# Weights ahead of batch 0, kv in the banks of the turned queries, gated relu chunks: one change to a cosformer attention kernel

## The chip, the cores and the metric

The kernel runs on one core of one Trainium2 chip. The metric is the device time of one execution in microseconds (us). A run is called slow when it is over 1.5% above the fastest of the same kernel.

PE is the matmul engine and PEld its weight load. DVE is the vector engine, ACT the scalar engine, and Pool the GpSimd engine, which here also issues the loads. A "turn" is a transpose by matmul: the result appears in PSUM, the memory that PE writes, and another engine copies it into SBUF. A name like L281 is a line of the kernel that the text speaks of; the same statement has another number in each kernel.

## The reference

Linear attention with cosine and sine weights over 8 batches, then a feed-forward layer with softplus, cut to what matters:

```python
# q, k, v: (8 batches, 8 heads, 576 positions, 64)
q_p, k_p = phi(q), phi(k)     # phi: relu, then [r * cos(pos), r * sin(pos)]
kv  = einsum('bhsf,bhsd->bhfd', k_p, v)
z   = k_p.sum(over positions)
x   = (q_p @ kv) / (q_p @ z + 1e-6)            # 4608 tokens of 512
h   = x @ w_in                                 # 512 -> 2048
out = (maximum(h, 0) + log1p(exp(-abs(h)))) @ w_out
```

Where every h is small, the last line is close to `ln 2 * sum(w_out) + x @ (w_in @ w_out) / 2`. The kernel computes that: it folds the two weights into one 512 x 512 matrix `W_c`. It squares x and w_in to check at the end that h was small enough, and holds a slow branch for the other case.

## The kernel before

The 4608 tokens are 36 tiles of 128. Two batches of 576 make nine tiles: four of each, and one that holds the last 64 tokens of both. A batch's work:

```python
def relu(b):                                   # once a batch, on Pool
    nc.gpsimd.tensor_copy(gate, vcs_bufs[(b - 1) % 2][:, 3, T - 1, 1, VW - 2 :])
    for hq in range(2):
        relu_q(b, hq, nc.gpsimd)               # q_sb -> q_r, a pool of 2 buffers
    relu_k(b, nc.gpsimd)

def turn_queries(b, n):                        # nine times a batch
    ...
    ps = qt_ps.tile([128, 512], F32, tag="qt") # qt_ps: bufs=2, one bank each
    ...                                        # two matmuls with diag (cos and sin) into ps
    nc.scalar.copy(dst, ps.rearrange("p (j c s) -> p j c s", j=2, c=4))

def key_values(b, hq):                         # twice a batch
    kv = big_ps.tile([128, 2, 512], F32, tag="big", name="kv_ps")   # shared with attend
    ...                                        # 36 matmuls, then two ACT copies into blk
```

The `gate` copy reads the last value that a scaling wrote, and the relu stands behind it on Pool. So Pool's relu starts after that scaling on DVE: in the trace of before, a gate copy waits 4.96 us for the scaling and runs at 62.80, and the relu follows at 62.95. And the main loop, one tile at a time:

```python
for j, i in enumerate(mine):
    attend(i)                                  # q.kv, q.z; DVE divides: x
    for hq, c in itertools.islice(scales, 2 if j == 0 else 1):
        scale_values(b + 1, hq, c)             # v * cos, v * sin on DVE
    if j == 2 and b + 2 < B:
        relu(b + 2)
    if more and j >= last - 1:
        key_values(b + 1, j - last + 1)
    some(1)                                    # a query turn of batch b + 1
    if i - 1 >= 4:
        turn_x(i - 1)                          # x turned, copied by ACT, squared by ACT
    some(1 if j < last else 9)
    if i - 2 >= 4:
        emit(i - 2)                            # x @ W_c + bias, stored
```

Batch 0 and its four tiles come first, while the weights arrive. Then come all squares and the fold of the weights, then batch 1.

Of the kernel before, what the change touches and what calls it, by code (L numbers as in the profile page):

```python
# [21 lines left out]
def kernel(  # L22
# [19 lines left out]
    T = 9  # L42
# [11 lines left out]
    qt_ps = ctx.enter_context(tc.tile_pool(name="qt_ps", bufs=2, space=PSUM))  # L54
# [4 lines left out]
    def view(ap, *dims, offset=0):  # L59
        return bass.AP(  # L60
            tensor=ap.tensor, offset=ap.offset + offset,
            ap=[list(ap.ap[0])] + [list(d) for d in dims],
        )

# [12 lines left out]
    warm = singles.tile([128, 512], BF16)  # L77
    nc.vector.memset(warm, 1.0)
    load(0, "q", 0)
    load(0, "q", 1)  # L80


    idx_i = singles.tile([128, T], mybir.dt.int32)
# [4 lines left out]
    for part in range(2):  # L88
        load(0, "k", part)
        load(0, "v", part)  # L90

    xT_all = singles.tile([128, N_TOK // 128, KO, 128], BF16)
    w_in_sb = xT_all[:, 4 : 4 + D_FF // 128].rearrange("p n g t -> p (n g t)").rearrange(
        "p (ko f) -> p ko f", ko=KO
    )
    w_out_sb = singles.tile([128, FO, D_MODEL], BF16)
    for ko in range(KO):
        nc.gpsimd.dma_start(w_in_sb[:, ko, :], moe_w_in[ko * 128 : (ko + 1) * 128, :])
    w_out_r = moe_w_out.rearrange("(fo p) m -> p fo m", p=128)
    for f in range(0, FO, 4):  # L100
        nc.gpsimd.dma_start(w_out_sb[:, f : f + 4, :], w_out_r[:, f : f + 4, :])
    for b in (1, 2, 3):
        for name in ("q", "k", "v"):
            load(b, name)

    ones = singles.tile([128, 128], F32)
    nc.vector.memset(ones, 1.0)
    blk_bufs = []
    for r in range(3):
        blk = singles.tile([128, 2, 2, 2, C], BF16, name=f"kvblk{r}")  # L110
        nc.vector.memset(blk, 0.0)
        blk_bufs.append(blk)
# [11 lines left out]
    nc.scalar.copy(cs_wide, view(cs_col, [1, 2 * T], [0, D]))  # L124
    diag = singles.tile([128, T, 2, 128], BF16)
    for t in range(T):
        for c in range(2):
            nc.vector.tensor_scalar_mul(diag[:, t, c, :], ident, cs_col[:, c, t : t + 1])
    perm = singles.tile([128, 128], BF16)
    nc.vector.tensor_copy(view(perm, [2, 64], [1, 2]), view(ident, [1, 64], [64, 2]))  # L130
# [5 lines left out]
    def turn_w_in(ko, half):  # L136
        n = (2 * ko + half) % 3
        pool, tag = (xt_ps, "xt") if n == 0 else (qt_ps, "qt")
        ps = pool.tile([128, 8, 128], BF16, tag=tag, name="wT_ps")
        for j in range(8):  # L140
            ft = 8 * half + j
            nc.tensor.matmul(
                ps[:, j, :], w_in_sb[:, ko, ft * 128 : (ft + 1) * 128], ident,
                is_transpose=True, start=True, stop=True, skip_group_check=True,
            )
        dst = view(
            w_inT, [D_MODEL, 8], [128, 2], [1, 64],
            offset=8 * half * D_MODEL + 256 * (ko // 2) + 64 * (ko % 2),
        )
        src = ps.rearrange("p f (h d) -> p f h d", h=2)  # L150
        if half:
            nc.scalar.copy(dst, src)  # L152
        else:
            nc.vector.tensor_copy(dst, src)

    def fold(pair, quarter, ps):
        for ft in range(4 * quarter, 4 * quarter + 4):
            for j in range(2):
                g = 2 * pair + j
                nc.tensor.matmul(  # L160
                    ps[:, j, :], w_inT[:, ft, g * 128 : (g + 1) * 128], w_out_sb[:, ft, :],
                    start=(ft == 0), stop=(ft == FO - 1),
                )
# [32 lines left out]


    VW = D + 2
    vcs_bufs = []
    for r in range(2):  # L200
        vcs = singles.tile([128, 4, T, 2, VW], BF16, name=f"vcs{r}")
        vcs_bufs.append(vcs)

    def mark_values(r):
        for hp in range(4):
            at = 0 if hp % 2 else D
            nc.vector.tensor_copy(
                vcs_bufs[r][:, hp, :, :, at : at + 2], view(cs_col, [1, T], [T, 2], [0, 2])
            )

    def scale_values(b, hq, c):
        vcs = vcs_bufs[b % 2]
        nc.vector.tensor_mul(  # L213
            view(vcs, [T * 2 * VW + 2, 2], [2 * VW, T], [1, D],
                 offset=2 * hq * T * 2 * VW + c * VW),
            kqv[b, "v"][:, 2 * hq : 2 * hq + 2],
            view(cs_wide, [0, 2], [D, T], [1, D], offset=c * T * D),
        )

    def key_values(b, hq):  # L220
        vcs, blk, k_r = vcs_bufs[b % 2], blk_bufs[b % 3], kqv[b, "k"]
        kv = big_ps.tile([128, 2, 512], F32, tag="big", name="kv_ps")
# [18 lines left out]
    TURNS = [(hq, tp) for tp in range(TP) for hq in range(2)] + [(0, TP)]  # L241

    def turn_queries(b, n):
        hq, tp = TURNS[n]
        q_r = q_rs[b]
        if n == 0:
            qTs[b] = work.tile([128, 2, 4, S], BF16, tag="qT", name="qT", bufs=3)
        qT = qTs[b]
        ps = qt_ps.tile([128, 512], F32, tag="qt")
# [10 lines left out]
        nc.scalar.copy(dst, ps.rearrange("p (j c s) -> p j c s", j=2, c=4))  # L260


    tiles = []
    for b in range(B):
        tiles += [[(b, 128 * tp, 128, 0)] for tp in range(TP)]
        if b % 2:
            tiles.append([(b - 1, 512, 64, 0), (b, 512, 64, 64)])
    xs = {}

    x_norm = singles.tile([128, len(tiles)], F32)  # L270
    w_norm = singles.tile([128, FO], F32)

    def attend(n):
        num = big_ps.tile([128, 4, 256], F32, tag="big", name="num_ps")
        for g in range(4):
# [12 lines left out]
        x = outs.tile([128, 4, 2, D], BF16, tag="x", bufs=3)  # L288
        nc.vector.tensor_mul(  # L289
            x, view(num, [256, 4], [66, 2], [1, D]), view(rden, [2, 4], [1, 2], [0, D])  # L290
        )
        xs[n] = x

    def turn_x(n):
        x = xs.pop(n)
        ps = xt_ps.tile([128, 4, 128], F32, tag="xt", name="xT_ps")
        for g in range(4):
            nc.tensor.matmul(  # L298
                ps[:, g, :], x[:, g, :, :], perm if len(tiles[n]) == 1 else ident, start=True, stop=True, skip_group_check=True,
            )  # L300
        nc.scalar.copy(xT_all[:, n], ps)  # L301
        square = outs.tile([128, D_MODEL], BF16, tag="square", name="square", bufs=1)
        nc.scalar.activation(square, x, ACT.Square, bias=zero_b, accum_out=x_norm[:, n : n + 1])  # L303
# [9 lines left out]
    def emit(n):  # L313
        ps = o_ps.tile([128, D_MODEL], F32, tag="o", name="o_ps")
# [7 lines left out]
    def spin(count):  # L322
        ps = qt_ps.tile([128, 512], F32, tag="qt", name="spin_ps")
        for _ in range(count):
            nc.tensor.matmul(ps, warm[:, :128], warm, start=True, stop=True, skip_group_check=True)

    def fetch(b):
        for name in ("q", "k", "v"):
            load(b, name)

    gate = singles.tile([128, 2], BF16)

    def relu(b):

        nc.gpsimd.tensor_copy(gate, vcs_bufs[(b - 1) % 2][:, 3, T - 1, 1, VW - 2 :])  # L335
        for hq in range(2):
            relu_q(b, hq, nc.gpsimd)
        relu_k(b, nc.gpsimd)

    spin(16)  # L340
    for hq in range(2):
        relu_q(0, hq, nc.vector)
    mark_values(0)
    for hq in range(2):
        relu_k(0, nc.vector, slice(2 * hq, 2 * hq + 2))
        for c in range(2):
            scale_values(0, hq, c)
    for n in range(9):
        turn_queries(0, n)
    key_values(0, 0)  # L350
    spin(2)
    key_values(0, 1)
    spin(2)
    w_turns = iter([(ko, half) for ko in range(KO) for half in range(2)])
    for n in range(4):
        attend(n)
        turn_w_in(*next(w_turns))
        if n:
            turn_x(n - 1)
    mark_values(1)  # L360
    for ko, half in w_turns:
        turn_w_in(ko, half)
        if (ko, half) == (2, 0):
            turn_x(3)
    for ft in range(FO):
        square = outs.tile([128, D_MODEL], BF16, tag="square", name="square", bufs=1)
        nc.scalar.activation(  # L367
            square, w_inT[:, ft, :], ACT.Square, bias=zero_b, accum_out=w_norm[:, ft : ft + 1]
        )
    wc_ps = [big_ps.tile([128, 2, D_MODEL], F32, tag="big", name=f"wc_ps{r}") for r in range(2)]  # L370
    for quarter in range(4):
        sum_w_out(quarter)
        for pair in range(2):
            fold(pair, quarter, wc_ps[pair])
    for hq in range(2):
        relu_q(1, hq, nc.vector)
# [3 lines left out]
    bias()  # L380
    relu_k(1, nc.vector)
    for n in range(9):
        turn_queries(1, n)
        if n % 2:
            emit(n // 2)
            scale_values(1, n // 4, n // 2 % 2)
    for hq in range(2):
        key_values(1, hq)
    fetch(4)
    relu(2)  # L390

    n = 4
    for b in range(1, B):
        mine = [i for i in range(n, len(tiles)) if tiles[i][-1][0] == b]
        last = len(mine) - 1
        more = b + 1 < B
        turns = iter(range(9))

        def some(count):
            for _ in range(count):  # L400
                t = next(turns, None) if more else None
# [112 lines left out]
```

## Time and profile before

| | before |
|---|---|
| median of the first 3 runs | 149.9 us (149.88 to 150.5) |
| span of the profiled run, granted clock | 148.7 us, 0.971 |
| busy: PE, DVE, ACT, Pool | 81%, 73%, 76%, 36% |
| loads done | about 108 us |
| nine tiles in the middle | 24.45 us |
| x of tiles 0, 4, 9, 18, 27, 31, 35 starts at | 17.9, 53.3, 68.4, 92.8, 117.3, 129.0, 136.2 us |

The last row follows one DVE instruction, the multiplication that makes x, through the timeline. It happens once a tile, so it serves as the tiles' clock.

### The profile page before, as it was taken

How to read it: one execution, taken by the hardware profiler on the slowest of the kernel's cores; microseconds unless marked ns; L12 is line 12 of the kernel's file. 1: busy time of each engine (PE TensorE's matmuls, PEld its weight loads, DVE VectorE, ACT ScalarE, POOL GpSimd, SP SyncE). 2: the span in 40 equal slices, each digit the busy share in tenths (PEclk: the TensorE clock that was granted, in tenths of full speed). 3: DMA queues.
4: the chain of work that ended last, by engine and by line, in shares of the span. 5: the costliest groups of instructions: out<-in, count | busy, mean ns of one | idle time of the engine just before them, and what ended most of it. 6: DMA issues, size and time to landing. Idle time of an engine off the chain costs nothing.

```text
span 148.7 us, 3802 instructions
## 1 busy us (share of the span) xinstructions
PE 119.9 (81%) x1482; PEld 75.6 (51%) x1482; DVE 108.9 (73%) x237; ACT 113.7 (76%) x255; POOL 53.0 (36%) x67
## 2 busy tenths in 40 slices
PE   6966875999967728798979899897899988999510
PEld 2323665444434507566657567575567755664100
DVE  6867494699467579978967986994998798599420
ACT  3468298999995626899899889989988989967300
POOL 6965132231300095196079059219009200000000
PEclk9999999999999986999999999999999999999985
DMA  1999999999999999999999999999942324144430
GB/s 21 181 179 216 213 213 202 209 204 209 207 207 208 267 266 209 208 208 265 239 250 256 239 239 269 228 256 249 241 171 82 142 74 109 61 155 152 153 90 4
DMA packets 20678, 28.07 MB, mean 189 GB/s; under 512 B 1200, under 2 KB 15536, under 8 KB 20656
## 3 DMA queue, kind: packets, MB, share of 16 engines
q0 software_dynamic: 15408, 18.35, 71.8%
q1 hardware_dynamic: 5248, 9.44, 18.8%
q8 instruction: 12, 0.20, 0.5%
q14 instruction: 10, 0.08, 0.2%
HBM read 36.70 MB, written 9.44 MB: 310 GB/s over the span
## 4 chain that ended last, share of the span: by engine, by line
PE 33%; DVE 25%; ACT 23%; issue 7%; DMA 5%; POOL 3%; DVEq 0%; POOLq 0%
PE o_ps L316 17%; DVE o_sb L318 11%; ACT square L367 9%; DVE vcs L213 8%; DMA v_sb<-in_v_dram 5%; PE kv_ps L227 5%; PE num_ps L279 4%; PE ps L252 4%; DVE x L289 3%; ACT square L303 3%; ACT qT L260 3%; ACT w_inT L152 3%; PE xT_ps L298 2%; ACT xT_all L301 2%; ACT kvblk L234 2%
## 5 line engine op out<-in xcount | busy, mean ns | idle before, releaser
L260 ACT CAST qT<-ps 128x512 bf16<-128x512 f32 x72 | 40.6, 592 | 11.3 <-PE ps L252 10.9
L316 PE MATMUL o_ps<-W_c,xT_all 128*128 128x512 bf16 x144 | 36.9, 378 | 5.1 <-DVE o_sb L318 3.5
L318 DVE TENSOR_TENSOR o_sb<-o_ps,b_bc 128x512 f32<-128x512 f32 x36 | 24.8, 688 | 13.4 <-PE o_ps L316 13.3
L252 PE MATMUL ps<-diag,q_r 128*128 128x256 bf16 x144 | 27.7, 279 | 8.1 <-ACT qT L260 4.6
L213 DVE TENSOR_TENSOR vcs<-v_sb,cs_wide 128x1152 bf16<-128x1152 bf16 x32 | 27.9, 871 | 2.4 <-ACT qT L260 1.2
L289 DVE TENSOR_TENSOR x<-num_ps,rden 128x512 bf16<-128x512 f32 x36 | 24.9, 692 | 3.3
L303 ACT ACTIVATE square<-x,zero_b 128x512 bf16<-128x512 bf16 x36 | 26.6, 739 | 0.0
L279 PEld LDWEIGHTS <-qT 128*128 128x128 bf16 (+1 forms) x320 | 19.6, 101 | 9.0 <-DVE x L289 1.9
L279 PE MATMUL num_ps<-kvblk,qT 128*128 128x130 bf16 (+1 forms) x320 | 23.4, 223 | 0.6 <-ACT kvblk L234 0.5
L301 ACT CAST xT_all<-xT_ps 128x512 bf16<-128x512 f32 x36 | 21.5, 596 | 3.0 <-PE xT_ps L298 3.0
L316 PEld LDWEIGHTS <-xT_all 128*128 128x128 bf16 x144 | 13.8, 97 | 17.1 <-issue 7.9
L252 PEld LDWEIGHTS <-q_r 128*128 128x128 bf16 x144 | 11.8, 99 | 15.0 <-issue 8.0
L234 ACT CAST kvblk<-kv_ps 64x260 bf16<-64x260 f32 x32 | 12.0, 375 | 6.0 <-PE kv_ps L227 5.7
L298 PE MATMUL xT_ps<-perm,x 128*128 128x128 bf16 x128 | 12.6, 222 | 3.0 <-DVE x L289 1.2
L160 PE MATMUL wc_ps<-w_out_sb,w_inT 128*128 128x512 bf16 x64 | 14.0, 379 | 0.1
L192 POOL TENSOR_SCALAR q_r<-q_sb 128x1152 bf16<-128x1152 bf16 x12 | 13.6, 1145 | 0.0
L298 PEld LDWEIGHTS <-x 128*128 128x128 bf16 x144 | 10.8, 99 | 5.3 <-issue 2.1
L227 PE MATMUL kv_ps<-vcs,k_sb 64*64 64x132 bf16 x576 | 11.5, 219 | 2.1 <-DVE vcs L213 2.0
L187 POOL TENSOR_SCALAR k_sb<-k_sb 128x2304 bf16<-128x2304 bf16 x6 | 12.6, 2102 | 0.0
L73 POOL DMA_DIRECT2D k_sb<-in_k_dram x9 | 6.7, 739 | 16.1 <-PE kv_ps L227 10.7
L367 ACT ACTIVATE square<-w_inT,zero_b 128x512 bf16<-128x512 bf16 x16 | 11.6, 723 | 0.5
L335 POOL COPY gate<-vcs 128x2 bf16<-128x2 bf16 x6 | 1.1, 190 | 29.1 <-DVE vcs L213 29.1
(55 smaller groups left out, 115.4 us busy)
## 6 DMA issues: line engine op xcount, KB each, us to landing
out_dram<-o_sb SPq DMA_DIRECT2D x32, 256.0 KB, 5.9
q_sb<-in_q_dram POOLq DMA_DIRECT2D x7, 576.0 KB, 20.5
k_sb<-in_k_dram POOLq DMA_DIRECT2D x7, 576.0 KB, 18.5
v_sb<-in_v_dram POOLq DMA_DIRECT2D x7, 576.0 KB, 20.9
xT_all<-in_moe_w_in_dram POOLq DMA_DIRECT2D x4, 512.0 KB, 12.6
w_out_sb<-in_moe_w_out_dram POOLq DMA_DIRECT2D x4, 512.0 KB, 18.5
out_dram<-o_sb SPq DMA_DIRECT2D x8, 128.0 KB, 4.0
q_sb<-in_q_dram POOLq DMA_DIRECT2D x2, 288.0 KB, 5.0
```

Source lines behind the costliest of these rows:

```text
L213: nc.vector.tensor_mul(view(vcs, [T * 2 * VW + 2, 2], [2 * VW, T], [1, D], offset=2 * hq * T * 2 * VW + c * VW), kqv[b, "v"][:, 2 * hq : 2 ...
L227: nc.tensor.matmul(kv[64 * i : 64 * i + 64, h2, : 2 * VW], k_r[rows, 2 * hq + i, t, :], vcs[rows, 2 * hq + i, t, :, :], start=(t == 0), st ...
L252: nc.tensor.matmul(ps[:, 256 * j : 256 * j + 256], q_r[:, hj, t, :, :], diag[:, t, :, :], start=True, stop=True, skip_group_check=True,)
L260: nc.scalar.copy(dst, ps.rearrange("p (j c s) -> p j c s", j=2, c=4))
L279: nc.tensor.matmul(num[p0 : p0 + m, g, :C], qTs[b][:, hq, 2 * c + h2, t0 : t0 + m], blk_bufs[b % 3][:, h2, hq, c, :], start=(c == 0), stop ...
L289: nc.vector.tensor_mul(x, view(num, [256, 4], [66, 2], [1, D]), view(rden, [2, 4], [1, 2], [0, D]))
L298: nc.tensor.matmul(ps[:, g, :], x[:, g, :, :], perm if len(tiles[n]) == 1 else ident, start=True, stop=True, skip_group_check=True,)
L301: nc.scalar.copy(xT_all[:, n], ps)
L303: nc.scalar.activation(square, x, ACT.Square, bias=zero_b, accum_out=x_norm[:, n : n + 1])
L316: nc.tensor.matmul(ps, xT_all[:, n, g, :], W_c[:, g, :], start=(g == 0), stop=(g == 3))
L318: nc.vector.tensor_add(o_sb, ps, b_bc)
L367: nc.scalar.activation(square, w_inT[:, ft, :], ACT.Square, bias=zero_b, accum_out=w_norm[:, ft : ft + 1])
```

## The change

The intent has five parts. The weights come first, in eight blocks, with batch 0 after the fifth, so that turns, squares and fold go on beside the loads. Query turns are spread two a tile. kv accumulates in the two banks of the turned queries, so that it takes no buffer from the attention sums. Squares cover two tiles at once. A value scaling and a Pool relu chunk, with its gate, come one per tile, so that they do not meet. The core of the diff:

```diff
-    qt_ps = ctx.enter_context(tc.tile_pool(name="qt_ps", bufs=2, space=PSUM))
+    qt_ps = ctx.enter_context(tc.tile_pool(name="qt_ps", bufs=1, space=PSUM))
+    banks = qt_ps.tile([128, 2, 512], F32)
+    turn_no = [0]
...
+    load_w(0)
...
+    for j in range(1, 5):
+        load_w(j)
+    for name in ("k", "v", "q"):
+        for part in range(2):
+            load(0, name, part)
+    for j in range(5, BLOCKS):
+        load_w(j)
...
+    def pool_relu(b, part, after):
+        hq, c = part // 2, part % 2
+        nc.gpsimd.tensor_copy(gate, vcs_bufs[after % 2][:, 2 * hq + 1, T - 1, c, VW - 2 :])
+        if part < 2:
+            relu_k(b, nc.gpsimd, slice(2 * part, 2 * part + 2))
+        else:
+            relu_q(b, part - 2, nc.gpsimd)
...
-        kv = big_ps.tile([128, 2, 512], F32, tag="big", name="kv_ps")
+        kv = banks
...
-        ps = qt_ps.tile([128, 512], F32, tag="qt")
+        ps = banks[:, turn_no[0] % 2]
+        turn_no[0] += 1
...
+            turns[len(tiles)] = [(b, tp, hq) for hq in range(2)]
+            tiles.append([(b, 128 * tp, 128, 0)])
         if b % 2:
+            turns[len(tiles)] = [(b - 1, TP), (b, TP)]
             tiles.append([(b - 1, 512, 64, 0), (b, 512, 64, 64)])
...
+            for part in itertools.islice(parts, (0, 1, 2, 1)[j] if b == 0 else left < 4):
+                scale_values(b + 1, part)
+                if b + 2 < B:
+                    pool_relu(b + 2, part, b + 1)
+            attend(i)
...
+    emit(last - 1, big_ps)
+    emit(last, big_ps)
```

## The prediction

The sum, 40.5 + 31 x 2.6 + 4 x 2.05 + 12.3 + 1.2, came to 142.8 us, given as 142.5.

> **What bounds the kernel now.** I read four views in this order: the page's 40 slices (where it is dense), the busy time by stretch (what one batch costs), the timeline of the first 63 us (what delays the start), and the end of the timeline.
>
> The slices, each 3.72 us; DMA is the mean busy share of the DMA engines:
> ```profile
> DVE  6867494699467579978967986994998798599420
> ACT  3468298999995626899899889989988989967300
> DMA  1999999999999999999999999999942324144430
> GB/s 21 181 179 216 213 213 202 209 204 209 207 207 208 267 266 209 208 208 265 239 250 256 239 239 269 228 256 249 241 171 82 142 74 109 61 155 152 153 90 4
> ```
> DMA is full from the second slice to about 108 us and then nearly idle, so the stream of loads ends 40 us before the kernel does. Without stores it writes about 209 GB/s of bf16. The page counts 18.35 MB written by loads, of which a batch (9 x 64 x 4 x 128 x 2 bytes, three times) is 1.77 MB: 8.5 us. Loads alone are about 88 us.
>
> The busy time by stretch, two periods of two batches (9 tiles each) in the middle:
> ```profile
> core 0: us, PE busy (x) PEld busy (x) DVE busy (x) ACT busy (x) POOL busy (x), PEclk, DMA share, GB/s
> 62.30:86.75 24.45, 22.31 (x336) 15.47 (x340) 20.03 (x45) 22.92 (x54) 13.41 (x14) 1.00 1.18 240
> 86.75:111.20 24.45, 22.30 (x337) 15.49 (x340) 19.89 (x45) 22.79 (x54) 11.19 (x11) 1.00 1.05 235
> ```
> Two equal periods of 24.45 us, so 2.72 us a tile, at full TensorE clock. ACT is busy 93% and PE 91%, with pipelined latency counted in. There is no single wait to remove: ACT's queue and the query turns that wait for its copies set the beat.
>
> The timeline of the first part:
> ```profile
> 16.55 0.74 POOL L73 DMA_DIRECT2D q_sb<-in_q_dram  x1 [1.71 <-DMA xT_all<-in_moe_w_in_dram]
> 26.65 13.97 PE L160 MATMUL wc_ps<-w_out_sb,w_inT 128*128 128x512 bf16 x64
> 40.57 0.72 ACT L367 ACTIVATE square<-w_inT,zero_b 128x512 bf16<-128x512 bf16 x1
> 42.89 1.02 PE L316 MATMUL o_ps<-W_c,xT_all 128*128 128x512 bf16 x4 [0.98 <-ACT b_bc L180]
> 51.50 0.41 PE L279 MATMUL num_ps<-kvblk,qT 128*128 128x130 bf16 x4
> 53.50 2.28 POOL L192 TENSOR_SCALAR q_r<-q_sb 128x1152 bf16<-128x1152 bf16 x2
> 53.90 5.36 DVE L213 TENSOR_TENSOR vcs<-v_sb,cs_wide 128x1152 bf16<-128x1152 bf16 x2
> ```
> The weights' fold (64 matmuls, 14 us) starts only at 26.7 us, after all turns of the weights; beside it ACT works off 16 squares until 41.3 us. Only then come batch 1's turns, mixed with the four late outputs of batch 0, and attention resumes with tile 4 at 51.5 us. Right after, two value scalings of 0.75 us take 5.36 us beside Pool's relu.
>
> The end of the timeline:
> ```profile
> 135.02 0.66 PE L279 MATMUL num_ps<-kvblk,qT 128*64 128x130 bf16 x16
> 137.68 1.02 PE L316 MATMUL o_ps<-W_c,xT_all 128*128 128x512 bf16 x4 [0.30 <-DVE o_sb L318]
> 140.54 0.69 DVE L318 TENSOR_TENSOR o_sb<-o_ps,b_bc 128x512 f32<-128x512 f32 x1 [1.11 <-PE o_ps L316]
> ```
> The last tile's attention starts at 135.02 us, 13.7 us before the span ends at 148.7.
>
> [...] ACT copies of 1024 and 512 columns take 1014 and 592 ns, so 0.82 ns a column. [...] The loads read f32 and write bf16, so 209 GB/s written is 418 read[...]. [...] The trace has a granted clock of 0.83 between 50 and 60 us, where PE is busy 56%.
>
> **The change, part by part.**
>
> *Head.* Weights come first in eight blocks, batch 0 after five. Total bytes are the same. In before, the first 512 KB weight block (2.29 MB into the stream) frees its queue slot at 16.55 us; at 206 GB/s this fits a landing at 5.5 us + bytes/206. So block 5 of 8 lands at 18.2, k, v, q of batch 0 at 21.1, 24.0, 26.8, and the last weights at 34.5 us, as before. What changes is the work waiting then. Turns, squares and fold go block by block (fold 8 x 0.216 = 1.7 us, turns 0.6 us, per 2.5 us of arrival), so squares are hidden. But PE's order puts block 5 behind batch 0's turns (about 30 us)[...]. I get fold 5 done about 35.5, folds 6 and 7 by 39.5, then about 1 us until the first half of the sums has left PSUM. **Tile 0 starts at about 40.5 us.** The old kernel has tile 4 at 51.5; the new one should have it at 40.5 + 4 x 2.6 = 50.9. So the head by itself gains almost nothing: the gain is that the batch-1 hole (51.5 to 62, four tiles at about 2.7 us) is gone and the rhythm is better.
>
> *ACT in the loop.* Start to start, a query copy takes 0.48 us, a turned-x copy 0.48, a square with its accumulator read 0.71, a kv copy 0.385. A batch has 9, 4.5, 4.5 and 4: 4.3 + 2.2 + 3.2 + 1.5 = 11.2 of 12.2 us. The change squares two tiles at once: 0.71 + 512 x 0.82 ns = 1.13 for two instead of 1.42, so 0.65 us less a batch: 10.55. The cs_wide copy (1.15) and the four weight copies (3.9) go to DVE, in the head, where they cost nothing I can see.
>
> *DVE in the loop.* A tile takes 0.2 + 0.3 + 0.61 + 0.6 = 1.7 us start to start, a scaling about 0.67: 4.5 x 1.7 + 4 x 0.7 = 10.5 us a batch, unchanged. Batch 1's relu (1.4 + 0.75) leaves DVE for Pool.
>
> *PE in the loop.* Output 0.87, turns 4 x 0.11, attention 0.46, x 0.22 a tile and 1.3 a batch for kv: about 10.3 us, unchanged. But query turns are now spread two a tile instead of bunched at the batch's end, where PE waited 2.6 us for ACT in those two periods, and kv no longer takes a buffer of the attention sums. In return kv takes both query banks: it waits for the last query copies, and the next turns for kv's own copies (0.76). I put that at some 0.4 us twice a batch.
>
> *Beat.* ACT, DVE and PE then all have about 10.5 us of work a batch. With the old slack of about 1 us this is 11.5 us: 2.57 a tile. The DMA allows no better: 8.6 us of loads plus 4.5 stores, each about 0.63 us of its time (from 5.6 MB stored beside 12.4 MB loaded in the 73.5 us from 34.5 to 108), is 11.4 us. I take **2.6**.
>
> *Tail.* Tiles 31 to 35 had 1.81 us each; now some turns remain, so about 2.05, +1 us. The last two outputs no longer share one bank (o_sb, then 1.0 of matmul, then 0.7): 1.4 us less, so 12.3 from the last attention to the end.
>
> *Sum.* 40.5 + 31 x 2.6 = 121.1 for tile 31; + 4 x 2.05 = 129.3 for tile 35; + 12.3 = 141.6 of span; + 1.2 (149.9 - 148.7) = 142.8. I say 142.5 us.
>
> **Rivals.**
> A. *The banks serialise.* If kv in the query banks costs more than I put, say 3.2 us in each kv tile, the beat stays 2.7: 145.9 us. For: ACT's copies already end a wait of PE. Against: kv lost its wait for an attention buffer.
> B. *DMA is the bound.* The last batch lands at about 110 us (34.5 + 7 x 8.6 + 0.63 x 25 tiles stored). If the loop could run at 2.4 us, it would stand waiting there; tile 31 not before about 117: 138.5. For: three engines at 10.5. It is the floor, so it gives the low end. [...]
> C. *Pool meets DVE again.* Pool's relu for batch b+2 is ordered behind a scaling, but by B that batch's q lands late, so Pool starts when data lands, not when DVE is done. Four chunks of 1.1 us in 11.5 make a hit likely for one or two of four scalings: about 1 us of DVE a batch, beat 2.65 to 2.7: 144 to 146.
> D. *The load stream hides all.* If only the order of loads mattered, the time would stay near 149.9. Against: the stream ended 40 us before the end.
>
> **Range and chances.** Low end from B, 138.5; high end from A with C, 147.5. Faster by over 2% means under 146.9; that fails only if beat and head both go wrong, so 0.87; same 0.11; slower 0.02.
>
> **What would show it.** First attention at 39 to 42 us and W_c before it; loads ending at 108 to 112 us; a period of 9 tiles of 23 to 24 us with ACT's busy time near 21.5; the longest vcs about 1.8 us, not 4.5; the last attention 12.3 us before the end. The prediction is wrong if the head ends past 44 us[...], if kv's waits for query copies exceed 1 us each, or if scalings take over 1.2 us on average.

## More of the kernel before

The view of waits gives, for each pair of an engine's line and what released it, the time waited in all, how often, and the longest. Of the kernel before, the two lines on its query turns are

```profile
ACT qT L260 <- PE ps L252: 10.9, 10, 3.2
PE ps L252 <- ACT qT L260: 4.6, 9, 0.8
```

The two query buffers let PE turn into one while ACT empties the other. Of 72 turns only 9 waited for ACT, 4.6 us together.

## The result, and the profile after

The changed kernel takes 192.62 us (190.39 to 194.39, 4 runs), against 150.2 us (149.88 to 150.6, 4 runs) of the kernel before in the same rounds. The ratio of fast runs is 1.2731, interval 1.2641 to 1.2821. A ratio is the mean time of one kernel's fast runs over that of the other's of the same rounds, so it is not quite the ratio of the medians. The change is 27% slower, and the prediction of 142.5 us is off by 50 us.

The profiled run of after is a slow one: 194.39 us, span 192.5, clock 0.884. With two further executions, three of six count as fast (190.39, 191.15 and 192.2, clocks of 0.882 to 0.901). Their mean, 191.2 us, is 1 to 2% shorter than the profiled run, and is what the differences below start from. What is read below is over ten times that size.

The page of after, the 40 slices, each 4.81 us:

```profile
PE   5689354946866837868869448786776869867940
ACT  3265132653565742467685426878872467788520
POOL 7975446087800196462000866530066300000000
PEclk9999955897996995589987988999998599999996
DMA  4999999999997149989811299999121111312350
```

DMA is full to about 58 us. Then it has holes in the middle of the loads, and just before and in each hole Pool is idle too. In or just after the first two holes PE falls to 3 and 4 and ACT to 2. So no load rate and no busy engine sets the end: something stands still. TensorE's clock reads 5 in the two slices after the first hole; after the second it reads 8.

The groups of instructions, the same view of the page as before (busy time, mean ns | idle before and what ended it):

```profile
L289 ACT CAST qT<-banks 128x512 bf16<-128x512 f32 x70 | 40.9, 585 | 31.5 <-PE banks L281 31.4
L281 PE MATMUL banks<-diag,q_r 128*128 128x256 bf16 x144 | 31.0, 302 | 26.3 <-ACT qT L289 24.2
L243 DVE TENSOR_TENSOR vcs<-v_sb,cs_wide 128x1152 bf16<-128x1152 bf16 x32 | 28.4, 891 | 13.2 <-POOL gate L235 13.1
L225 POOL TENSOR_SCALAR q_r<-q_sb 128x1152 bf16<-128x1152 bf16 x14 | 16.1, 1148 | 42.0 <-PE banks L281 28.2
```

Each copy takes what it took before (585 and 592 ns), and a turn's matmul little more (302 and 279 ns, at a clock of 0.884 in place of 0.971). What grew is the idle time ahead of them. The view of waits has the same as counts:

```profile
ACT qT L289 <- PE banks L281: 31.4, 37, 3.4
...
POOL q_r L225 <- PE banks L281: 28.2, 2, 14.2
...
PE banks L281 <- ACT qT L289: 24.2, 43, 1.0
...
DVE vcs L243 <- POOL gate L235: 13.1, 4, 4.9
```

Two things are new. Query turns now wait for ACT's copies 43 times, 24.2 us, where they waited 9 times, 4.6 us. And Pool's relu of q stands twice for 14 us until a query turn is done.

The busy time by stretch (stretch, length, then busy us of PE, PEld, DVE, ACT and Pool, the granted clock, DMA share and GB/s), for a stretch of nine tiles (8 to 17) and one of ten (17 to 27):

```profile
80.30:119.00 38.70, 27.32 (x345) 17.66 (x340) 21.45 (x45) 22.91 (x44) 14.61 (x22) 0.88 0.72 149
119.00:157.10 38.10, 28.82 (x379) 18.99 (x368) 23.80 (x50) 25.66 (x51) 12.73 (x20) 0.91 0.54 129
```

The work of nine tiles on ACT and DVE is much as in before (22.9 and 21.5 us in the first stretch, 22.9 and 20.0 in before), and PE's is longer at the lower clock (27.3 at 0.88, in before 22.3 at 1.00). But that stretch is 38.7 us long in place of 24.45. Over the 27 tiles from 4 to 31, x starts every 4.04 us.

**The first stall, in the timeline** (start, duration, engine, instruction, [idle before <- releaser]), four turns between tiles 3 and 4:

```profile
57.33 0.38 PE L281 MATMUL banks<-diag,q_r 128*128 128x256 bf16 x2 [0.67 <-ACT qT L289]
57.75 0.59 ACT L289 CAST qT<-banks 128x512 bf16<-128x512 f32 x1 [0.47 <-PE banks L281]
58.38 0.38 PE L281 MATMUL banks<-diag,q_r 128*128 128x256 bf16 x2 [0.67 <-ACT qT L289]
58.80 0.59 ACT L289 CAST qT<-banks 128x512 bf16<-128x512 f32 x1 [0.47 <-PE banks L281]
```

The turn at 57.33 writes one half of `banks`, the next at 58.38 the other. Yet it starts only when the copy out of the first half has ended at 58.34. PE and ACT take turns, 1.05 us a piece, as if there were one buffer.

**The second stall**, Pool's relus of q with a long wait ahead:

```profile
66.87 1.15 POOL L225 TENSOR_SCALAR q_r<-q_sb 128x1152 bf16<-128x1152 bf16 x1 [14.06 <-PE banks L281]
...
106.39 1.15 POOL L225 TENSOR_SCALAR q_r<-q_sb 128x1152 bf16<-128x1152 bf16 x1 [14.18 <-PE banks L281]
...
141.42 1.15 POOL L225 TENSOR_SCALAR q_r<-q_sb 128x1152 bf16<-128x1152 bf16 x1 [12.21 <-DVE o_sb L351]
```

Three waits, 40.5 us together, one for every two batches; the view puts the third down to DVE, not to a turn. Then the instructions that stood behind the first of them follow:

```profile
69.19 0.79 POOL L77 DMA_DIRECT2D k_sb<-in_k_dram  x1
71.70 1.69 DVE L243 TENSOR_TENSOR vcs<-v_sb,cs_wide 128x1152 bf16<-128x1152 bf16 x1 [4.87 <-POOL gate L235]
73.54 1.20 PE L257 MATMUL banks<-vcs,k_sb 64*64 64x132 bf16 x36 [4.38 <-DVE den L315]
```

Pool issues the next batch's load only at 69.19, with a DMA share of 0.14 from 62 to 67 us. DVE's scaling waited 4.87 us for Pool's gate copy, and PE waited 4.38 us until kv could start.

**The start** in after, between the end of the fold and the first attention:

```profile
40.50 2.19 DVE L206 TENSOR_TENSOR w_sum<-w_sum,w_tmp 128x1024 f32<-128x1024 f32 x1
42.72 0.69 DVE L208 TENSOR_TENSOR w_tmp<-w_sum 128x512 f32<-128x512 f32 x1
43.33 1.28 DVE L392 TENSOR_SCALAR W_c<-wc_ps 128x512 bf16<-128x512 f32 x2
44.07 0.62 PE L309 MATMUL num_ps<-kvblk,qT 128*128 128x130 bf16 x8 [3.17 <-DVE W_c L392]
```

The first attention starts at 44.07 us, not 40.5. PE had been ready 3.17 us; the sums of w_out come first on DVE, one of them at 2.19 us where it took 1.23 in before (and 1.23 in after too, at 37.16, with Pool waiting; that Pool's relu beside the longer one is the cause was not tried), and only then the copies that free the attention's buffers.

### The profile page after: what moved, and what is told of

The parts are those of the page before. It is cut to its first block, busy times and chain, and to the rows that moved or that the text cites. A ratio compares the mean times of both kernels' runs of the same rounds, so it can differ in the third digit from the quotient of the medians.

```text
span 192.5 us, 3782 instructions
## 1 busy us (share of the span) xinstructions
PE 132.3 (69%) x1473; PEld 83.1 (43%) x1473; DVE 115.6 (60%) x249; ACT 107.5 (56%) x212; POOL 71.8 (37%) x107
## 4 chain that ended last, share of the span: by engine, by line
PE 39%; ACT 19%; DVE 17%; POOL 10%; issue 7%; DMA 5%; POOLq 0%; DVEq 0%
PE o_ps L349 14%; PE banks L281 10%; ACT qT L289 10%; ACT warm L188 6%; DVE vcs L243 6%; PE num_ps L309 5%; PE banks L257 5%; DMA xT_all<-in_moe_w_in_dram 5%; POOL q_r L225 3%; PE xT_ps L329 3%; DVE w_sum L206 2%; DVE w_tmp L204 2%; DVE o_sb L351 2%; POOL xT_all L99 2%; POOL w_out_sb L100 1%
## 5 line engine op out<-in xcount | busy, mean ns | idle before, releaser
L289 ACT CAST qT<-banks 128x512 bf16<-128x512 f32 x70 | 40.9, 585 | 31.5 <-PE banks L281 31.4
L281 PE MATMUL banks<-diag,q_r 128*128 128x256 bf16 x144 | 31.0, 302 | 26.3 <-ACT qT L289 24.2
L351 DVE TENSOR_TENSOR o_sb<-o_ps,b_bc 128x512 f32<-128x512 f32 x34 | 23.4, 689 | 26.2 <-PE o_ps L349 25.9
L281 PEld LDWEIGHTS <-q_r 128*128 128x128 bf16 x144 | 14.7, 106 | 38.7 <-issue 36.0
L264 ACT CAST kvblk<-banks 64x260 bf16<-64x260 f32 x32 | 12.0, 374 | 29.8 <-PE banks L257 29.6
L309 PE MATMUL num_ps<-kvblk,qT 128*128 128x130 bf16 (+1 forms) x320 | 24.8, 237 | 3.2 <-DVE W_c L392 3.2
L257 PE MATMUL banks<-vcs,k_sb 64*64 64x132 bf16 x576 | 13.7, 245 | 17.8 <-DVE den L315 12.5
L309 PEld LDWEIGHTS <-qT 128*128 128x128 bf16 (+1 forms) x320 | 21.2, 109 | 10.9 <-issue 6.1
L188 ACT ACTIVATE warm<-x,zero_b 128x1024 bf16<-128x1024 bf16 x18 | 20.7, 1151 | 0.0
L257 PEld LDWEIGHTS <-k_sb 64*64 64x64 bf16 x576 | 11.3, 122 | 20.2 <-POOL k_sb L220 12.2
L220 POOL TENSOR_SCALAR k_sb<-k_sb 128x1152 bf16<-128x1152 bf16 x14 | 16.3, 1162 | 4.3 <-DMA k_sb<-in_k_dram 4.3
L188 ACT ACTIVATE warm<-w_inT,zero_b 128x512 bf16<-128x512 bf16 x16 | 11.5, 722 | 10.4 <-DVE w_inT L182 10.1
L235 POOL COPY gate<-vcs 128x2 bf16<-128x2 bf16 x28 | 7.7, 276 | 20.2 <-DVE vcs L243 13.8
L315 DVE TENSOR_SCALAR den<-num_ps 128x8 f32<-128x8 f32 x36 | 5.8, 160 | 12.7 <-PE num_ps L309 12.6
```

The costliest lines, as they stand in the source:

```text
L188: nc.scalar.activation(warm[:, :size], source, ACT.Square, bias=zero_b, accum_out=dst)
L257: nc.tensor.matmul(kv[64 * i : 64 * i + 64, h2, : 2 * VW], k_r[rows, 2 * hq + i, t, :], vcs[rows, 2 * hq + i, t, :, :], start=(t == 0), st ...
L281: nc.tensor.matmul(ps[:, 256 * j : 256 * j + 256], q_r[:, hj, t, :, :], diag[:, t, :, :], start=True, stop=True, skip_group_check=True,)
L289: (copy or nc.scalar.copy)(dst, ps.rearrange("p (j c s) -> p j c s", j=2, c=4))
L309: nc.tensor.matmul(num[p0 : p0 + m, g, :C], qTs[b][:, hq, 2 * c + h2, t0 : t0 + m], blk_bufs[b % 3][:, h2, hq, c, :], start=(c == 0), stop ...
L351: nc.vector.tensor_add(o_sb, ps, b_bc)
```

## The experiments

Two theories stood at the start, and a third for the rest.

- **A, one tile.** `banks` is one tile of two banks. The accesses to both halves are ordered as if they were one, so a turn into one half waits for the copy out of the other: 0.67 us ahead of a turn in the timeline above.
- **B, the late column.** The ninth query turn of an even batch (its last 64 positions) moved to the shared tile, a batch later. It still reads `q_r`, of which there are two buffers. Pool's relu for two batches on needs that buffer and waits, and in Pool's order the fetches and gates wait behind it.
- Rivals: the loads, kv in the query banks, or a lower TensorE clock by itself.

### e1_two_tiles: the two banks as two tiles

```diff
-    banks = qt_ps.tile([128, 2, 512], F32)
+    banks = [qt_ps.tile([128, 512], F32, name=f"bank{r}") for r in range(2)]
...
-        ps = banks[:, turn_no[0] % 2]
+        ps = banks[turn_no[0] % 2]
```

kv still uses both, so its two copies of two banks become four of one.

> The changed kernel, with the two banks as two separate PSUM tiles instead of two halves of one, and kv's copies out of them four of 64x130 instead of two of 64x260; nothing else. Theory A (the halves of one tile are ordered against each other, so each query turn waits for the copy of the turn before it): about 190 falls to 160 to 170 us, and the wait of query turns for ACT's query copies falls from 24 us to under 6. Theory B (Pool stands behind a q buffer that is freed a batch too late, and loads and scalings stand behind Pool): stays above 180 us, with Pool's relu of q still waiting over 10 us for the turns.

Measured: 169.31 us (167.22 to 170.15); the two fast runs are 168.57 and 167.22, and there are too few for a ratio. The profile is a fast one. Its DMA slices, each 4.17 us, and then two lines of its waits:

```profile
DMA  3999999999999992999999379999951131413360
```
```profile
POOL q_r L225 <- PE bank L282: 29.7, 3, 10.1
...
DVE vcs L243 <- POOL gate L235: 12.5, 4, 4.9
```

Turns no longer wait for the copies in any amount that the list of the largest waits shows; before the edit it was 24.2 us. Pool's three waits remain, shorter (29.7 us in place of 40.5), and so do the gate's. A is a cause, worth 23.3 us here (the mean of fast runs, 191.2 against 167.9), and not the only one.

### e2_early_turn: the late column a batch earlier

```diff
             turns[len(tiles)] = [(b, tp, hq) for hq in range(2)]
+            if b % 2 == 0 and tp == TP - 1:
+                turns[len(tiles)].append((b, TP))
...
-            turns[len(tiles)] = [(b - 1, TP), (b, TP)]
+            turns[len(tiles)] = [(b, TP)]
```

> The changed kernel, with the ninth column of an even batch's queries turned with that batch's own fourth tile, not with the shared tile a batch later, so that its relu'd queries are free a batch earlier; one tile of two banks as in the changed kernel. Theory A: stays above 175 us. Theory B: falls to 160 to 170 us, Pool's wait for query turns goes from 28 us to under 5, and DMA is dense until about 120 us.

Measured: 171.37 us (170.45 to 173.1), ratio 1.1367 (1.1314 to 1.142). The DMA slices, each 4.24 us, and two lines of the waits:

```profile
DMA  3999999999999999949978996997132212113360
```
```profile
PE banks L281 <- ACT qT L289: 22.7, 40, 1.0
...
POOL q_r L225 <- DMA q_sb<-in_q_dram: 1.7, 1, 1.7
```

Pool's waits for a query turn are gone, the relu of q waits only 1.7 us for data, and the large DMA holes are gone. What is left are the turns that wait for ACT, 22.7 us of the 24.2. So B is a second cause, worth 20.1 us (191.2 against 171.1), and the two are separate: each edit takes away its own wait and leaves most of the other's.

### e3_both: both mends

The edits of e1_two_tiles and e2_early_turn together, nothing else.

> Both edits together: two PSUM tiles and the early turn. If A and B are all of the loss: 140 to 148 us, what was predicted for the change. If a third cause is left (the gate copy on Pool that orders scalings and relu[...]), above 150 us.

Measured: 154.60 us (154.41 to 155.57), ratio 1.0303 (1.0256 to 1.0349). The DMA slices (each 3.82 us), the busy time by stretch for a period of nine tiles, and the timeline where the turns ahead of tile 4 are bunched:

```profile
DMA  2999999999999999999999999999933133232450
```
```profile
64.50:89.00 24.50, 22.41 (x332) 15.81 (x331) 19.93 (x45) 21.84 (x51) 14.81 (x22) 1.00 1.16 239
```
```profile
57.07 0.60 PE L282 MATMUL bank<-diag,q_r 128*128 128x256 bf16 x4
57.49 2.81 ACT L290 CAST qT<-bank 128x512 bf16<-128x512 f32 x5
```

DMA is dense, the clock is at 1.00 in the loop, and five copies follow each other without a gap in 2.81 us, 0.56 each in place of 1.05. Of the 41.0 us by which after is slower than before (191.2 against 150.2), A and B together are 36.4 (191.2 against 154.8). Alone they gave 23.3 and 20.1, so about 7 us goes away with either edit: e1_two_tiles, which leaves B, has 10.8 us less of Pool's waits.

The rates of the loads and kv in the query banks are still there in this kernel, so neither is in those 36.4 us. But e3_both is 4.4 us above the kernel before, and 12 above the prediction. By tiles, in us:

| x starts at | tile 0 | tile 4 | tile 9 | tile 18 | tile 27 | tile 31 | tile 35 | span |
|---|---|---|---|---|---|---|---|---|
| before | 17.9 | 53.3 | 68.4 | 92.8 | 117.3 | 129.0 | 136.2 | 148.7 |
| predicted (attention + 1.2) | 41.7 | 52.1 | | | | 122.3 | 130.5 | 141.6 |
| after | 45.2 | 61.4 | 85.3 | 122.9 | 157.1 | 170.6 | 181.4 | 192.5 |
| e3_both | 44.9 | 60.0 | 73.1 | 97.9 | 122.1 | 133.3 | 141.8 | 152.8 |

The predicted row is the prediction's times of attention plus 1.2 us, the step from the last attention to its x in the trace of before (135.02 to 136.2). e3_both loses 3.2 us by tile 0, 7.9 by tile 4, and 11.0 by tile 31. Its nine tiles take 24.2 to 24.8 us, like before's. Against before it is 6.7 us late at tile 4, 4.3 at tile 31 and 4.1 at the end: what the mended change still loses, it loses ahead of tile 4.

### e4_before_one_tile: A alone, in the kernel before

```diff
-        ps = qt_ps.tile([128, 512], F32, tag="qt")
+        ps = banks[:, turn_no[0] % 2]
+        turn_no[0] += 1
```

`banks` is one tile of two banks as in after. The turns of the weights, which used the old buffers, go through two others.

> The kernel before, with its two query buffers made halves of one PSUM tile, used in turn, and the turned weights put through the two other single buffers; kv stays in the large buffers, nothing else of the change. Theory A: the turns wait for the copies in this kernel too, at least 0.5 us a turn over most of 72 turns: 165 to 180 us. Theory B: within 3 us of before.

Measured: 180.34 us (178.62 to 181.66), ratio 1.1936 (1.186 to 1.2012). Its view of waits:

```profile
PE banks L256 <- ACT qT L264: 25.9, 37, 1.3
ACT qT L264 <- PE banks L256: 24.6, 33, 3.3
```

The same alternation, with nothing else of the change there: neither kv in the banks, nor new loads, nor gates. 25.9 us of PE's waits in place of 4.6, and 30 us of time. Of these 30 us, 11.5 are there by tile 4, where the moved turns of the weights can have a part; 17.8 come between tiles 4 and 31 (93.5 us in place of 75.7), where only the query turns' buffers differ. The low clock comes with it (0.91 in its fast runs), without any other part of the change, and in e3_both's loop it is at 1.00, so it needs no cause of its own.

### e5_no_gate: Pool's gate taken away

```diff
-        nc.gpsimd.tensor_copy(gate, vcs_bufs[after % 2][:, 2 * hq + 1, T - 1, c, VW - 2 :])
```

On e3_both, for the rest. At its start DVE's scaling waits for the gate copy, which stands on Pool behind a relu and three issues of loads. Pool and then DVE in the timeline of e3_both:

```profile
46.22 1.14 POOL L225 TENSOR_SCALAR q_r<-q_sb 128x1152 bf16<-128x1152 bf16 x1
47.31 0.79 POOL L77 DMA_DIRECT2D k_sb<-in_k_dram  x1
...
49.57 0.22 POOL L235 COPY gate<-vcs 128x2 bf16<-128x2 bf16 x1
```
```profile
49.82 2.36 DVE L243 TENSOR_TENSOR vcs<-v_sb,cs_wide 128x1152 bf16<-128x1152 bf16 x2 [2.55 <-POOL gate L235]
```

> The kernel with both mends (two PSUM tiles, early turn), without the small gate copy that holds each Pool relu back until a scaling is done. Theory C1 (the gate is the third cause, since a scaling waits for the gate copy of the part before and that stands behind Pool's relu): 154.6 falls to 150 or less, and the scalings' wait for the gate, 2.6 us, is gone. Rival C2 (the gate costs nothing, it keeps Pool off VectorE): same within 1.5 us or slower, with scalings above 783 ns on average.

Measured: 155.91 us (155.16 to 157.12), ratio 1.0383 (e3_both: 1.0303). Tile 4's x comes at 56.6 us, 3.4 earlier. Tile 18 is 0.6 earlier, at 97.3, and tile 35 0.9 later, at 142.7. Its groups of instructions:

```profile
L242 DVE TENSOR_TENSOR vcs<-v_sb,cs_wide 128x1152 bf16<-128x1152 bf16 x32 | 31.7, 995 | 0.1
...
L220 POOL TENSOR_SCALAR k_sb<-k_sb 128x1152 bf16<-128x1152 bf16 x14 | 18.2, 1321 | 4.6 <-DMA k_sb<-in_k_dram 4.5
```

The scalings take 995 ns in place of 783, and Pool's relus of k 1321 in place of 1152: both engines take longer. So the theory that the gate's wait costs time in the end falls; what the gate costs at the start it saves in the loop. The gate's purpose, to keep the relu away from the scalings, was sound: in the trace of before, two scalings that start at 53.90, with Pool's relu running from 53.50, take 5.36 us, where one at 44.63 took 0.75.

### e6_scale_earlier: the scalings a tile earlier

```diff
-            for part in itertools.islice(parts, (0, 1, 2, 1)[j] if b == 0 else left < 4):
+            for part in itertools.islice(parts, (0, 2, 2, 0)[j] if b == 0 else (0, 1, 1, 2, 0)[left]):
                 scale_values(b + 1, part)
...
+            for part in itertools.islice(relus, (0, 1, 2, 1)[j] if b == 0 else left < 4):
+                pool_relu(b + 2, part, b + 1)
```

On e3_both. There PE's kv waits 10.2 us in all for the scalings.

> The kernel with both mends, where the four value scalings of a batch are done a tile earlier (two in the fourth tile from the end, one in each of the next two, none in the last), Pool's relu parts where they were. Theory C2 (one scaling per tile puts the last scaling into the same tile as the kv product that needs it, so TensorE waits for VectorE, 10.2 us in the profile): falls by 3 to 7 us, to 148 to 151.5, and kv's wait for scalings to under 4 us. C1, or a bound by DMA: same within 1.5 us.

Measured: 156.57 us (154.53 to 157.53), ratio 1.0359. kv's waits for a scaling fall from 10.2 to 4.6 us, but no time is won. The group of the scalings:

```profile
L243 DVE TENSOR_TENSOR vcs<-v_sb,cs_wide 128x1152 bf16<-128x1152 bf16 x32 | 31.4, 981 | 0.8
```

Moved, the scalings take 981 ns on average in place of 783, and Pool's relus of k 1210 in place of 1152. A miss. The longer scalings are the same sign as in e5_no_gate; that they are what ate the gain was not tried apart.

### e7_sum_last: the last sum of w_out behind the copies of W_c

```diff
-        if j > 0 and j % 2 == 0:
+        if j > 0 and j % 2 == 0 and j < BLOCKS:
...
+            if i == 0:
+                sum_w_out(3)
```

On e3_both, for the 3 us ahead of the first attention.

> The kernel with both mends, where the last sum over the rows of w_out (for the bias) is taken after the product's copies out of PSUM and after the first attention, not before them. The first attention starts 2 to 4 us earlier than 43.4 us. If the start of the loop sets the end, the time falls by as much, to 151 to 152.5; if the loads set it, the time stays within 1 us.

Measured: 157.01 us (154.95 to 158.32), half of the runs slow; fast ones 154.95 to 156.01, ratio 1.0344. In the profiled run, a slow one, tile 0 has its x at 41.5, 3.4 us earlier than e3_both, as intended. But tile 3 is at 57.3 (55.5 in e3_both) and tile 4 at 63.6 (60.0). The early start is given back before batch 1. The run does not tell all of why: the sum only moved, and still keeps DVE for 4.0 us (42.09 to 46.1) ahead of tile 1's x. After it, Pool's order is as late as before: q_r starts at 43.97 when q has landed (44.44 in e3_both), and the gate ahead of the next two scalings comes at 49.99 (49.57).

### e8_before_pairs: squares of two tiles, in the kernel before

```diff
-        square = outs.tile([128, D_MODEL], BF16, tag="square", name="square", bufs=1)
-        nc.scalar.activation(square, x, ACT.Square, bias=zero_b, accum_out=x_norm[:, n : n + 1])
+        if n % 2:
+            ...                                # one square of 1024 over two tiles
```

> The kernel before with one part of the change alone: one square for two tiles (1024 columns) instead of one for each. The prediction's claim that ACT's work sets the beat: 0.65 us less a batch in six batches of the loop, so 146 to 148 us. Rival (the beat is set by waits of a chain through several engines, and ACT's time is only high beside it): 149 to 150.5.

Measured: 150.49 us (150.24 to 151.57), ratio 1.0015 (0.9974 to 1.0056): the same. The work did go away; these are the groups by form:

```profile
L306 ACT ACTIVATE square<-x,zero_b 128x1024 bf16<-128x1024 bf16 x18 | 20.9, 1162 | 0.0
...
L306 ACT ACTIVATION_READ_ACCUMULATOR square<-x,zero_b 128x1 f32 x18 | 3.6, 203 | 0.0
```

The squares alone take 20.9 us in place of 26.6, and its accumulator reads 3.6 in place of 7.4, yet no time was won. (A read's record is 203 ns long, but adds less: in after, where squares cover two tiles too, one starts at 85.95 and the next copy at 86.04.) The prediction's claim that ACT's queue, 93% busy, sets the beat falls.

### e9_kv_big and e10_kv_big_early: kv back in the attention's buffers

e9_kv_big is e3_both with kv of batches 1 to 7 in the buffers where it was before:

```diff
-        kv = banks
+        if b:
+            big = big_ps.tile([128, 2, 512], F32, tag="big", name="kv_ps")
+            kv = [big[:, h2] for h2 in range(2)]
+        else:
+            kv = banks
```

> The kernel with both mends, with kv of batches 1 to 7 accumulated in the large PSUM buffers again, as in the kernel before; batch 0's kv stays in the query banks. Theory D (kv in the query banks makes the two tiles of a batch that hold it cost about 3.1 us against 2.4 us of the others, since kv waits for the query copies and the next turns for kv's copies): nine tiles in 23 us instead of 24.5, and 154.6 falls to 149 to 152. Rival (kv in the large buffers holds up the attention sums as much): within 1 us of 154.6.

Measured: 153.55 us (153.2 to 153.91), ratio 1.0202 (1.0168 to 1.0235). The interval lies just under e3_both's, which is from other rounds (1.0235 against 1.0256), so kv in the query banks, with its four copies in place of two, costs about 1 to 1.5 us. Neither forecast was met. Its nine tiles take 24.4 and 23.5 us (74.1, 98.5, 122.0).

e10_kv_big_early is that with e6_scale_earlier's edit on top.

> As the run before, with the value scalings a tile earlier too. If kv's two waits (banks, scaling) only hide one another: 146 to 150 us. If VectorE's work sets the beat (a tile with a scaling takes 2.3 us of VectorE without a gap): within 1.5 us of the run before.

Measured: 156.51 us (152.07 to 157.22). Five of six runs are slow against the one of 152.07, so there is no result to use.

### e12_before_better: batch 1's scalings later, in the kernel before

Two tries for a better kernel start from before, both with the part of the change that held: the last two outputs in two buffers. This one also moves the two scalings that took 5.36 us.

```diff
-            for hq, c in itertools.islice(scales, 2 if j == 0 else 1):
+            for hq, c in itertools.islice(scales, (0, 0, 2, 1, 1)[j] if b == 1 else 2 if j == 0 else 1):
...
-    emit(n - 2)
-    emit(n - 1)
+    emit(n - 2, big_ps)
+    emit(n - 1, big_ps)
```

> The kernel before with two edits that its own trace asks for: batch 1's four value scalings two tiles later, so that they do not meet Pool's relu of batch 2 (two of them took 5.36 us), and the last two outputs in the large PSUM buffers, as the change has it. 3 to 4 us from the first and about 1.4 us from the second: 145 to 147 us, faster than both kernels. If the loop after it is bound by something that does not start earlier (loads): 148 to 149.

Measured: 152.78 us (152.15 to 154.05), ratio 1.0168, unclear at the limit of 2%. The end is shorter: 10.9 us from the last x to the end of the span, not 12.5. But the late scalings met the next relu on Pool, as the timeline shows:

```profile
57.92 0.18 POOL L338 COPY gate<-vcs 128x2 bf16<-128x2 bf16 x1
...
60.35 2.11 POOL L187 TENSOR_SCALAR k_sb<-k_sb 128x2304 bf16<-128x2304 bf16 x1
...
60.67 2.40 DVE L213 TENSOR_TENSOR vcs<-v_sb,cs_wide 128x1152 bf16<-128x1152 bf16 x1
```

Moving a scaling only moved the collision: this one takes 2.40 us where one at 50.17 took 0.75. A miss, and the edit made it: the gate now stands in the program ahead of the last scaling, whose value it reads, so it holds nothing back. It also ran ahead of two scalings that come before it in the program and write another part of the same `vcs` tile, in SBUF. So there two parts of one tile are not ordered as one; what theory A says was measured for the two banks of `banks` (24.2 us of waits in after, 25.9 in e4_before_one_tile), and does not hold for every tile.

### e13_before_vector_relu: batch 2's relu on DVE, in the kernel before

```diff
     fetch(4)
-    relu(2)
+    for hq in range(2):
+        relu_q(2, hq, nc.vector)
...
             attend(i)
+            if i == 4:
+                relu_k(2, nc.vector)
```

and the two buffers for the last outputs. This takes the collision away instead of moving it: one engine does both.

> The kernel before with batch 2's relu of q and k on VectorE, which stands idle for 2 us there (1.4 + 0.75 us of work), not on Pool, where it blocked two scalings for 3.8 us and held the first query turns; and the last two outputs in the large PSUM buffers, which in the last run took the time from the last tile's x to the end from 12.5 to 10.9 us. If both count: the sixth tile's x at about 56.5 us instead of 59.6, and 145 to 147.5 us, faster than both kernels. If only the end counts: 148.5 to 149.

Measured: 146.05 us (145.57 to 148.61), ratio 0.9723 (0.9673 to 0.9773): 2.8% faster than before, and the fastest kernel here. The profiled run is its one slow run. DVE in its timeline:

```profile
53.03 1.41 DVE L192 TENSOR_SCALAR q_r<-q_sb 128x1152 bf16<-128x1152 bf16 x2
...
56.22 0.75 DVE L187 TENSOR_SCALAR k_sb<-k_sb 128x2304 bf16<-128x2304 bf16 x1
56.89 1.55 DVE L213 TENSOR_TENSOR vcs<-v_sb,cs_wide 128x1152 bf16<-128x1152 bf16 x2
```

DVE needs 1.41 + 0.75 us for the relu that takes Pool 2.3 + 2.1, and the two scalings fall from 5.36 to 1.55 us. How its 4.2 us split between this and the end was not tried apart. In the slow profile, tile 0 to tile 9 takes 48.1 us in place of 50.5, and the end is 1.3 us shorter (135.6 to 146.8). Part may also come with the clock: four of the five fast runs have 0.985 to 0.994, where before's in the same rounds have at most 0.976. The fifth, at 0.964, took 147.41 us.

## Why the prediction was wrong, point by point

- **The step that failed most** is that of the banks. "In return kv takes both query banks ... I put that at some 0.4 us twice a batch" looked only at kv. It took for granted that the two halves of `banks` stay two buffers for the query turns, because they lie in two banks. The runs show that they did not: 43 waits, 24.2 us, in after; 23.3 us of time when they are two tiles (e1_two_tiles); and 25.9 us of waits and a ratio of 1.19 with one tile in the kernel before (e4_before_one_tile). Rival A, "the banks serialise", had the name but for kv alone, at 3.4 us on the whole time.
- **A step that was missing.** "But query turns are now spread two a tile" did not follow where the ninth turn went, and how long it holds `q_r`. It held up Pool in three waits of 12 to 14 us, and cost 20.1 us of time (e2_early_turn). Pool was taken for an engine with slack that waits only for loads (rival C); it issues the loads, so its stall became everybody's.
- **The head.** The first attention was put at 40.5 us and came at 44.07: past the 44 us that the prediction gave as a warning. The term "about 1 us until the first half of the sums has left PSUM" measured 3.17, behind DVE's sums. But e7_sum_last moved the last of these sums behind the first attention, and nothing was won.
- **The hole at batch 1.** The prediction saw the gain of the head in this, that "the batch-1 hole" was gone. It put the hole at four tiles of about 2.7 us, which is the old beat and no hole; in before, tiles 4 to 8 take 3.1 us each (53.3 to 65.7), with 6.3 us between tiles 4 and 5 alone. In e3_both these four take 9.8 us, but a new hole lies ahead of them: tiles 1 to 4 take 13.4 us (46.6 to 60.0) where 7.8 were put. There batch 1's relu of q starts when q has landed (44.44 us, after a wait of 1.69), and its values are scaled behind Pool's fetches and gates. The prediction put the weights ahead of batch 1 and did not ask when batch 1's own chain could start, though its own rate has batch 1 landed only at 43.1 (34.5 + 8.6). In before, q was the first of a batch's three loads, and batch 1's relu of q ran on DVE at 37.5. Without the gates, in e5_no_gate, tile 4 is 3.4 us earlier; the rest was not tried.
- **ACT sets the beat.** The saving was sized right. Two single squares were put at 1.42 us and a double one at 1.13, start to start; in after a double one takes 1.14 (84.90 to the next copy at 86.04). It was worth nothing (e8_before_pairs, ratio 1.0015).
- **A beat of 2.6 us.** After's was 4.04 over tiles 4 to 31. With both mends it is 2.71, that of before's nine-tile periods (2.72). The step was "all have about 10.5 us of work a batch" plus "the old slack of about 1 us" (11.5 us over 4.5 tiles is 2.56, not 2.57); adding busy times and a slack did not give the beat.
- **Rival B, the loads as floor**, was right in size: with the mends the loads end at about 110 us, as it had them. In after they did not set the end: they are done at about 135 us, with DMA at 4 or less in five of the sixteen slices from 58 us to there, and the last x comes 46 us later.
- **Right:** the load order and rate (DMA full to 58 us, about 200 to 209 GB/s from the fourth slice on; batch 1's q is there at 44.3 us, 1.2 later than by the prediction's rate, and why was not tried); the longest scalings (1.69 us singly in after, in place of 5.36 for two); and the end: 11.1 us from the last x in after, 12.5 in before, so the 1.4 us that were put for it. That the stream of loads was full is shown by the DMA row at 9, with 200 to 209 GB/s in the row below it; that no order of the loads could make it faster was not shown.

**Still open:** what holds nine tiles at about 24.5 us in before, e3_both and e8_before_pairs alike. Less work on ACT (e8_before_pairs) and an unhindered kv (e9_kv_big) made it at most 0.7 us shorter; earlier scalings (e6_scale_earlier) made it over an us longer (25.8). Several limits of nearly one size would look like this, but that is argued, not shown. The split of the last 12 us between start (7.9) and beat (3.1) is read from the tiles' times; no run removed the start's part with the rest kept. What ends the start ahead of tile 4 in e3_both is open too, beyond the gates' 3.4 us.

## What to carry to other kernels

When two buffers become two halves of one PSUM tile, look in the new trace, or in a build, at whether the second user still runs beside the first: in after and e4_before_one_tile being in different banks was not enough (24.2 and 25.9 us of waits). The trace of before had a hint: DVE's first copy into `W_c` starts at 41.90 us, after a wait that the view puts down to ACT's copy out of the other bank of the same PSUM tile. When a read of a buffer is moved later, count who needs that buffer next, and what else stands in the order of the engine that will wait, above all if it issues the loads. When an instruction is moved past a gate, look at what the gate still waits for (e12_before_better). Where two engines collide, giving both pieces of work to the faster one can pay where moving them apart does not: the ratios to before were 0.9723 in e13_before_vector_relu and 1.0168 in e12_before_better.
